# Attention, then a feed-forward layer: two further step orders, a fourth conversion buffer, a weight chunk asked for one period earlier

## The chip, the core and the metric

The kernel runs on one core of a Trainium2 chip. The metric is device time in microseconds (us). The engines are PE (TensorE), DVE (VectorE), ACT (ScalarE) and POOL (GpSimd); SP (SyncE) issues nearly all transfers. Each works through a queue of its own in the order in which the program was written, and waits at semaphores for what the others make.

## What is computed

```python
scores = 1/8 * matmul(q, k.T)                       # batch 8, heads 8, 576 tokens, head size 64
thresh = max(scores, -1) - tau                      # tau = 0.02
scores = where(scores >= thresh, scores, -1e9)
attn   = exp(scores - max(scores)); attn /= sum(attn) + 1e-9
x      = matmul(attn, v)                            # bridged to 4608 x 512
out    = maximum(x @ w_in, 0) ** 2 @ w_out          # 512 -> 2048 -> 512
```

q, k and v are float32. The two weight matrices come as float64, which the kernel takes as pairs of 32-bit words and turns into float32 itself.

## The kernel before

The first part of the run is attention, the rest is the feed-forward layer, which multiplies blocks with a scheme that needs sums of weight blocks beforehand. All of the change lies in the attention part.

**Units and periods.** Two heads form a pair (64 x 2 columns). 128 query rows of a pair, or the 64 leftover rows of two pairs, are a unit; there are 144 of them. A *period* p handles two units, A = 2p and B = 2p+1, so 72 periods are needed. A period's work is cut into named steps (`steps`, line 695). They are:

- PE: `SA`, `SB` scores against 512 keys and `RA`, `RB` against the last 64 (L434); `T` turns of q and k (L398); `U`, `V`, `W` turns of the finished weights of the softmax (L380); `Q` spreads the inverse sums (L517); `PV` multiplies by v (L534).
- DVE: `topA0` to `topB1` (L452) copy scores from PSUM and take the maximum; `maskA0` to `maskB1` (L467) compare with the threshold, multiply and sum, with two inputs in SBUF; `inv` (L477) is the reciprocal; `c4` (L227) and `c5` (L235) are two steps of a weight conversion; in periods without a conversion DVE also does half of `x` (L666).
- ACT: `powA0` to `powB1` (L462) are the exponentials; `eU`, `eV`, `eW` (L525) and `eT` (L403, L411) bring PE's turns from PSUM to SBUF; `x` (L664) copies the result; `c1` (L205) takes the absolute value of a chunk's high words.
- POOL: `leastA`, `leastB` (L459) make the thresholds; `over` (L474) adds 1e-9 to the sums; `xm` (L676) scales the result; `c2` (L212), `c3` (L219) and `c6` (L245) are conversion steps; `s1`, `s2` each do one sum of two weight blocks (L122, L125).
- SP: `fetch` (L191) asks for a chunk of raw weights; what `eT` and `xm` release is loaded and stored there too.

**The order.** Two strings list the steps: `CONVERTING` for the periods in which a weight chunk is in conversion (2 to 34) and `PLAIN` for the others; periods 0 and 1 have lists of their own (`BEGIN_WITH`, line 605). Each dash behind a name moves the step back by a period: `PV--` in period p is the `PV` of p-2. Since every engine works in order, the list fixes each engine's queue; waits between engines follow from the data, and from PSUM banks (`touch`, line 355: an access waits for the other engines' last one to the same bank). The scores use six banks: A's are 0 and 5, B's 2 and 3, the rests and the turns share 1 and 4; `W` and `Q` write to 2 and 3, `PV` to 0 and 5.

In the old plain order DVE does topB0, topB1, maskA1, x, inv, maskA0, maskB0, topA0, topA1, maskB1, and POOL s1, over, leastB, xm, s2, leastA. In the old converting order DVE does c5, topB1, c4, inv, topB0, maskA0, maskA1, topA0, topA1, maskB1, maskB0, and POOL c3, over, c6, leastB, xm, c2, leastA.

**Weight chunks.** 32 chunks are converted, one begun in each of the periods 2 to 33 (`starts`, line 564). A chunk's `fetch` stands two periods ahead of its `c1`; `c2` and `c3`, `c4`, `c5` and `c6` follow in that period and the next two. The raw words lie in one of four buffers, the absolute words (`a`, line 204) in one of three. From period 36 on `s1` and `s2` each make one sum, while there are any; `s2` only in periods before 60 (line 705).

Of the kernel before, what the change touches and what calls it, by code (L numbers as in the profile page):

```python
# [11 lines left out]
I32 = mybir.dt.int32  # L12
# [36 lines left out]
def kernel(  # L49
# [27 lines left out]
    P = 128  # L77
# [25 lines left out]
    sb, cv = Region(arena, 0, X_AT[0]), Region(arena, X_AT[0], ARENA)  # L103
# [49 lines left out]
    WC = 512  # L153
# [16 lines left out]
    blocks_out = [(m, k) for k in RAW for m in RAW]  # L170
    chunks += [(W_OUT, m, k, out_blocks[m, k]) for m, k in blocks_out[:EARLY]]
    is_wide = moe_w_in.dtype != FP32
    raws, parts = {}, {}

    def weight(m):
        return weight_tile(*chunks[m][0:3])

    def fetch(m):
        if m is None:
            return  # L180
        src = chunks[m][3]
        if not is_wide and m < 16:
            nc.sync.dma_start(out=weight(m)[:, :], in_=src)
            return
        raw = cv.tile([P, 2 * WC], I32, tag="raw", bufs=4, name="raw")
        if not is_wide:
            nc.sync.dma_start(out=raw[:, 0:WC].bitcast(FP32).rearrange("p (k o) -> p k o", k=4), in_=src)
            nc.sync.dma_start(out=slot_of(*chunks[m][1:3]), in_=raw[:, 0:WC].bitcast(FP32))
            return
        three = (lambda t: t.rearrange("p (k o) -> p k o", k=4)) if m >= 16 else (lambda t: t)  # L190
        nc.sync.dma_start(out=three(raw[:, :]), in_=src.bitcast(I32))  # L191
        raws[m] = raw

    def slot_of(m, k):
        return w_dram[ds((8 * raw_at(m) + raw_at(k)) * P, P), :]

    def pick(t, k):
        return t.rearrange("p (n two) -> p n two", two=2)[:, :, k]

    def convert1(m):  # L200
        if m not in raws:
            return
        lo, hi = pick(raws[m], 0), pick(raws[m], 1)
        a = cv.tile([P, WC], I32, tag="a", bufs=3, name="a")
        nc.scalar.activation(out=a.bitcast(FP32), in_=hi.bitcast(FP32), func=AF.Abs)  # L205
        parts[m] = (lo, hi, a)
        raws.pop(m)
# [280 lines left out]
    for g in range(2, 2 * len(pairs)):  # L488
        two, x = divmod(g - 4, 4)
# [9 lines left out]
    def fill(m, f, pt, at=None):  # L499

        first, count = FILLS[f]
        if m not in wT:
            wT[m] = sb.tile([P, (2 * CH + 2) * P], FP32, tag="wT", bufs=W_RING, name="wT")
        for i, (u, c) in enumerate(FIRST[first : first + count]):
            half_turn(pt, i, weights[2 * m + u][:, c, :, :].rearrange("p j d -> p (j d)"), at)
# [14 lines left out]
    def filled(m, f, pt, at=None):  # L520

        first, count = FILLS[f]
        count += 2 * (f == "W")
        to = wT[m][:, ds(weight_at(first) * P, count * P)]
        touch("weights", nc.scalar.copy(joined(to), whole(pt, 0, count)), at, 2 * BANK, m)  # L525
# [35 lines left out]
    def has(n):  # L561
        return 0 <= n < NU
# [5 lines left out]
    def sums_due(p):  # L568

        return p > max(starts) + 2 and not converts(p)  # L570

    def sums_step():
        while summing and next(summing[0], 0) == 0:
            summing.popleft()
# [10 lines left out]
    def converts(p):  # L585
        return is_wide and (has_chunk(p) or has_chunk(p - 1))
# [4 lines left out]
    def begun(n):  # L591
        return starts.get(n)

    FIRST_PERIOD = -2
    PLAIN = """
        c5- U-- SB-- c6 c4- eU-- RB-- s1- PV-- powA0-- topB0-- over-- topB1-- c1 powA1-- c2- powB0--
        maskA1-- T- x-- eT- leastB-- inv-- xm-- maskA0-- V-- W-- eV-- c3- Q-- eW-- powB1-- SA- maskB0-- RA-
        s2- topA0- topA1- maskB1-- leastA- fetch
    """.split()
    CONVERTING = """  # L600
        RB- RA eT- c5- topB1- powA0- c3- over- powA1- c6- fetch PV- x- powB1- c4 inv- topB0- leastB- V- eV-
        SA T W- xm- maskA0- powB0- maskA1- topA0 Q- eW- topA1 c2- maskB1- c1 U eU maskB0- SB leastA s1 s2
    """.split()

    BEGIN_WITH = {
# [2 lines left out]
        maskB0 maskB1  # L608
        """.split(),
        1: """  # L610
        fetch SA RA RB SB T eT over topA0 topA1 leastA inv V topB0 topB1 leastB powA0 powA1 eV W Q powB0 eW
        maskA0 maskA1 powB1 maskB0 maskB1
        """.split(),
    }
# [4 lines left out]
    def middle():  # L619
        return sc[:, 2 * BANK : 4 * BANK].rearrange("p (r n) -> p r n", r=2)  # L620

    def period(p):

        A, B_, a, b = 2 * p, 2 * p + 1, 2 * p - 2, 2 * p - 1
        m, turns = p - 2, TURNS.get(p, ())
        late, pt = {"W": []}, {}

        def fills(f, m):
            if has(2 * m):
                pt[f] = pt_pool.tile([P, 2, BANK], FP32, tag="pt", name="pt")  # L630
                fill(m, f, pt[f])

        def evict(f, m):
            if has(2 * m):
                filled(m, f, pt[f], 2 * BANK if f == "W" else None)

        def W():
            if has(2 * m + 2):
                pt["W"] = middle()
                fill(m + 1, "W", pt["W"], 2 * BANK)  # L640

        def Q():
            if has(2 * m + 2):
                spread_sums(m + 1, pt["W"], 2 * BANK)

        def turn_some():
            free = None
            if turns and p < 2:
                pq = pt_pool.tile([P, 2, BANK], FP32, tag="pt", name="pq")
                free = [(pq[:, r, :], None) for r in range(2)]  # L650
            late["turn"] = [turn(g // 2, g % 2, free or spots()) for g in turns]

        def PV():
            if has(2 * m):
                values(m)

        def values_out():
            if not has(2 * m):
                return
            late["x"] = x = sb.tile([P, 2, P], FP32, tag="x", bufs=2, name="x")  # L660
            for j in range(2):
                from_ = sc[:, ds(5 * j * BANK, P)]
                if converts(p) or j == 0:
                    made = nc.scalar.copy(x[:, j, :], from_)  # L664
                else:
                    made = nc.vector.tensor_tensor(  # L666
                        out=x[:, j, :], in0=from_, in1=wT[m][:, ts(SCALE_AT + j, P)], op=ALU.mult
                    )
                touch("x", made, 5 * j * BANK, P, m)

        def given_out():
            if has(2 * m):
                x = late.pop("x")
                made = x[:, 0 : 1 + converts(p), :].rearrange("p j n -> p (j n)")
                scale = wT[m][:, ds(SCALE_AT * P, (1 + converts(p)) * P)]
                nc.gpsimd.tensor_tensor(out=made, in0=made, in1=scale, op=ALU.mult)  # L676
                wT.pop(m)
                valued(m)
                give_x(m, x)
            ask(False)  # L680

        def scored(n):
            if has(n):
                scores(n, False)
                softmax(n)

        def scored_rest(n):
            if has(n):
                scores(n, True)

        def every(key):
            for then in late.get(key, ()):
                then()

        steps = {
            "U": lambda: fills("U", m), "V": lambda: fills("V", m + 1), "W": W, "Q": Q, "T": turn_some,
            "eU": lambda: evict("U", m), "eV": lambda: evict("V", m + 1), "eW": lambda: evict("W", m + 1),
            "eT": lambda: every("turn"),
            "SA": lambda: scored(A), "SB": lambda: scored(B_),
            "RA": lambda: scored_rest(A), "RB": lambda: scored_rest(B_),  # L700
            "PV": PV, "x": values_out, "xm": given_out,
            "c1": lambda: convert1(begun(p)), "c2": lambda: convert2(begun(p)),
            "c3": lambda: convert3(begun(p)), "c4": lambda: convert4(begun(p - 1)),
            "c5": lambda: convert5(begun(p - 1)), "c6": lambda: convert6(begun(p - 1)),
            "s1": lambda: sums_due(p) and sums_step(), "s2": lambda: sums_due(p) and p < 60 and sums_step(), "fetch": lambda: fetch(begun(p + 2)),
        }
        steps["over"] = lambda: do(a, "over")
        steps["inv"] = lambda: do(a, "inverse")
        for letter, n in (("A", A), ("B", B_)):
            for what, name in (("least", "least"),):  # L710
                steps[what + letter] = lambda n=n, name=name: do(n, name)
            for what, name in (("top", "top"), ("pow", "power"), ("mask", "mask")):
                for j in range(2):
                    steps[f"{what}{letter}{j}"] = lambda n=n, name=name, j=j: do(n, name, j)
        return steps
# [644 lines left out]
```

## Time and profile before

| what | value |
|---|---|
| three runs | 1295.56, 1300.23 and 1300.02 us, median 1300.02 |
| the profiled execution | 1296.16 us, of which the span is 1294.2 us |
| granted TensorE clock | 0.999 of full speed |
| PE busy | 1267.6 us, 98% of the span |
| DVE busy | 1000.9 us, 77% |
| ACT busy | 848.7 us, 66% |
| POOL busy | 1022.8 us, 79% |
| last reciprocal of the attention part | starts at 498.2 us |

The span runs from the first to the last instruction of the profiled execution; the run's own time is a little longer. "Busy" leaves out waiting, but an instruction that is held up after its start, for instance because another engine uses the same way to memory, counts as busy for all of its time. So one reads not only the gaps but also how long an operation takes in different places. In rows of the order in time, the columns are start, duration, engine, line, operation, output and input, shapes, count.

### The profile page before, as it was taken

How to read it: one execution, taken by the hardware profiler on the slowest of the kernel's cores; microseconds unless marked ns; L12 is line 12 of the kernel's file. 1: busy time of each engine (PE TensorE's matmuls, PEld its weight loads, DVE VectorE, ACT ScalarE, POOL GpSimd, SP SyncE). 2: the span in 40 equal slices, each digit the busy share in tenths (PEclk: the TensorE clock that was granted, in tenths of full speed). 3: DMA queues.
4: the chain of work that ended last, by engine and by line, in shares of the span. 5: the costliest groups of instructions: out<-in, count | busy, mean ns of one | idle time of the engine just before them, and what ended most of it. 6: DMA issues, size and time to landing. Idle time of an engine off the chain costs nothing.

```text
span 1294.2 us, 46028 instructions
## 1 busy us (share of the span) xinstructions
PE 1267.6 (98%) x18287; PEld 1103.2 (85%) x18287; DVE 1000.9 (77%) x2384; ACT 848.7 (66%) x1537; POOL 1022.8 (79%) x1070
## 2 busy tenths in 40 slices
PE   8999899999999999999999999999999999999998
PEld 5666666677777778988888888999999999999998
DVE  6999999999999995886887877877645654665463
ACT  6999999999999994666765766666523432443240
POOL 3999999988998542988897988758777867777775
PEclk9999999999999999999999999999999999999999
DMA  6655666444333312658767867589554324522411
GB/s 155 173 159 140 170 175 192 133 97 111 88 83 84 93 33 61 209 170 232 211 187 212 242 168 217 167 315 392 186 155 165 94 74 159 164 71 98 160 34 33
DMA packets 291414, 196.21 MB, mean 152 GB/s; under 512 B 100096, under 2 KB 252160, under 8 KB 291200
## 3 DMA queue, kind: packets, MB, share of 16 engines
q1 hardware_dynamic: 289888, 192.87, 51.3%
q8 instruction: 144, 2.36, 0.8%
q14 instruction: 70, 0.57, 0.1%
q10 hardware_dynamic: 1312, 0.41, 0.1%
HBM read 120.85 MB, written 72.35 MB: 149 GB/s over the span
## 4 chain that ended last, share of the span: by engine, by line
PE 68%; DVE 10%; DMA 7%; ACT 7%; issue 5%; POOL 2%; SPq 1%; DVEq 0%; ACTq 0%; POOLq 0%
PE po L1094 28%; PE ph L952 13%; PE sc L434 7%; PE ph L959 7%; PE sc L534 6%; DVE arena L452 4%; PE pt L380 3%; DVE arena L467 3%; DMA wall<-w 2%; ACT arena L525 2%; PE sc L398 1%; ACT arena L462 1%; PE sc L517 1%; DMA arena<-g 1%; DMA g<-arena 1%
## 5 line engine op out<-in xcount | busy, mean ns | idle before, releaser
L125 POOL TENSOR_TENSOR arena<-arena 128x512 f32<-128x512 f32 (+1 forms) x314 | 377.7, 1221 | 138.6 <-DVE arena L125 114.9
L1094 PE MATMUL po<-wall,arena 128*128 128x128 f32 x3528 | 395.2, 275 | 1.9 <-ACT arena L769 1.4
L1094 PEld LDWEIGHTS po<-wall,arena 128*128 128x128 f32 x3528 | 394.4, 192 | 2.6 <-ACT arena L769 1.8
L125 DVE TENSOR_TENSOR arena<-ph,arena 128x512 f32<-128x512 f32 x378 | 255.1, 689 | 79.0 <-PE ph L952 31.7
L122 POOL TENSOR_TENSOR arena<-arena 128x128 f32<-128x128 f32 (+1 forms) x322 | 265.8, 827 | 24.4 <-DMA arena<-w 8.8
L952 PE MATMUL ph<-arena,wall 128*128 128x256 f32 x1176 | 256.5, 380 | 2.2 <-DVE arena L125 1.8
L952 PEld LDWEIGHTS ph<-arena,wall 128*128 128x128 f32 x1176 | 222.2, 190 | 36.2 <-DVE arena L125 6.3
L467 DVE SCALAR_TENSOR_TENSOR arena<-arena 128x576 f32<-128x576 f32 x288 | 238.7, 848 | 3.4 <-ACT arena L462 0.5
L125 DVE TENSOR_TENSOR arena<-po,arena 128x128 f32<-128x128 f32 x378 | 108.3, 290 | 167.6 <-PE po L1094 163.1
L462 ACT ACTIVATE arena<-arena 128x576 f32<-128x576 f32 x288 | 216.0, 795 | 4.0 <-DVE arena L452 3.8
L808 ACT COPY c<-arena 128x512 f32<-128x512 f32 (+1 forms) x295 | 169.0, 578 | 73.7 <-DVE arena L122 35.8
L452 DVE TENSOR_SCALAR_CACHE_REDUCE arena<-sc 128x576 f32<-128x576 f32 x288 | 207.1, 747 | 8.5 <-ACT arena L525 3.4
L434 PE MATMUL sc<-arena 64*64 64x512 f32 (+1 forms) x2304 | 188.2, 418 | 7.9 <-ACT arena L403 1.5
L459 POOL TENSOR_SCALAR arena<-arena,tau_p 128x2 f32<-128x2 f32 x144 | 124.7, 866 | 78.4 <-DVE arena L452 71.5
L534 PE MATMUL sc<-arena 64*64 64x128 f32 (+1 forms) x5760 | 165.4, 260 | 0.1
L122 DVE TENSOR_TENSOR arena<-arena,c 128x512 f32<-128x512 f32 x235 | 154.4, 666 | 12.2 <-ACT c L808 8.7
L525 ACT COPY arena<-pt 128x1024 f32<-128x1024 f32 x144 | 146.9, 1020 | 7.3 <-PE pt L380 6.5
L534 PEld LDWEIGHTS sc<-arena 64*64 64x64 f32 x5760 | 150.4, 133 | 0.9 <-issue 0.4
L434 PEld LDWEIGHTS sc<-arena 64*64 64x64 f32 x2304 | 78.5, 133 | 83.5 <-issue 35.4
L769 ACT COPY arena<-po 128x128 f32<-128x128 f32 x63 | 16.6, 264 | 186.5 <-PE po L1094 183.7
L959 PE MATMUL ph<-arena,wall 128*128 128x128 f32 x1176 | 132.0, 275 | 0.6 <-DVE arena L666 0.6
L959 PEld LDWEIGHTS ph<-arena,wall 128*128 128x128 f32 x1176 | 131.6, 192 | 0.9 <-issue 0.7
(54 smaller groups left out, 1140.8 us busy)
## 6 DMA issues: line engine op xcount, KB each, us to landing
arena<-g SPq DMA_DIRECT2D x144, 256.0 KB, 4.5
g<-arena SPq DMA_DIRECT2D x192, 128.0 KB, 2.9
w<-arena SPq DMA_DIRECT2D x60, 256.0 KB, 2.6
wall<-w SPq DMA_DIRECT2D x49, 256.0 KB, 5.2
g<-arena SPq DMA_DIRECT2D x48, 256.0 KB, 3.6
arena<-w SPq DMA_DIRECT2D x44, 256.0 KB, 3.3
arena<-in_v_dram SPq DMA_DIRECT2D x32, 288.0 KB, 4.3
out_dram<-arena SPq DMA_DIRECT2D x70, 128.0 KB, 2.5
```

Of the source, the lines that this page charges most:

```text
L122: e.tensor_tensor(out=out, in0=x, in1=y, op=ALU.subtract)
L125: e.tensor_tensor(out=out, in0=x, in1=y, op=ALU.add)
L434: made = nc.tensor.matmul(sc[at, ds(to, count)], lhs, kT[rows, ds(at_k, count)], start=True, stop=True)
L452: made = nc.vector.tensor_scalar(out=s[:, j, :], in0=sc[:, ds(at, S)], scalar1=1.0, scalar2=None, op0=ALU.mult, op1=ALU.min, accum_out=nmx ...
L462: nc.scalar.activation(out=w[:, :, j, :], in_=of(j), func=AF.Exp, bias=nmx[:, j : j + 1], scale=-1.0)
L467: nc.vector.scalar_tensor_tensor(out=w[:, :, j, :], in0=of(j), scalar=thr[:, j : j + 1], in1=w[:, :, j, :], op0=ALU.is_le, op1=ALU.mult, a ...
L525: touch("weights", nc.scalar.copy(joined(to), whole(pt, 0, count)), at, 2 * BANK, m)
L534: made = nc.tensor.matmul(sc[ds(u * D, D), ds(5 * j * BANK + row, count)], loaded_v[i][rows, (c - (u != j)) % CH, :], wT[m][rows, ds(weigh ...
L808: nc.scalar.copy(c, y)
L952: nc.tensor.matmul(to[:, 2 * j : 2 * j + 2, :], W_IN[m, k][:, ts(2 * h + j, P)], part_x(steps, k, m), start=(not more and j == 0), stop=Tr ...
L959: nc.tensor.matmul(to[:, j, :], W_IN[m, k][:, ts(j, P)], x, start=(not more and j == 0), stop=True, skip_group_check=True,)
L1094: nc.tensor.matmul(to, g[:, j, :], w[:, j, :], start=(not more and j == 0), stop=(j == 3), skip_group_check=True)
```

## The change

Both lists of steps are replaced. A chunk's `c1` moves to the head of the converting period, so the absolute words get a fourth buffer. In period 1 a new step, `next`, asks for the chunk that would otherwise be asked for in period 2; `fetch` leaves out what has been asked for.

```diff
-    raws, parts = {}, {}
+    raws, parts, asked_for = {}, {}, set()
...
     def fetch(m):
-        if m is None:
+        if m is None or m in asked_for:
             return
+        asked_for.add(m)
...
-        a = cv.tile([P, WC], I32, tag="a", bufs=3, name="a")
+        a = cv.tile([P, WC], I32, tag="a", bufs=4, name="a")
...
     PLAIN = """
-        c5- U-- SB-- c6 c4- eU-- RB-- s1- PV-- powA0-- topB0-- over-- topB1-- c1 powA1-- c2- powB0--
-        maskA1-- T- x-- eT- leastB-- inv-- xm-- maskA0-- V-- W-- eV-- c3- Q-- eW-- powB1-- SA- maskB0-- RA-
-        s2- topA0- topA1- maskB1-- leastA- fetch
+        s2- PV-- x-- T-- V-- W-- c2 SA- c3- maskA0-- xm-- inv-- Q-- eT-- RB- maskB0-- topA0- c1- eV-- U-
+        topA1- leastA- eW-- SB- powB1-- maskB1-- eU- RA topB0- c4 topB1- s1 powA1- leastB- maskA1- over- c5
+        powA0- c6 powB0- fetch
     """.split()
     CONVERTING = """
-        RB- RA eT- c5- topB1- powA0- c3- over- powA1- c6- fetch PV- x- powB1- c4 inv- topB0- leastB- V- eV-
-        SA T W- xm- maskA0- powB0- maskA1- topA0 Q- eW- topA1 c2- maskB1- c1 U eU maskB0- SB leastA s1 s2
+        SB- c1 RA topB0- powA1- c2- topB1- PV- c5- powA0- maskA0- eT- leastB- over- V- x- T powB0- SA RB W-
+        maskA1- c3 c4 inv- Q- c6- fetch topA0 eV- topA1 leastA U xm- maskB0- powB1- eW- eU maskB1- s1 s2
     """.split()
...
         1: """
-        fetch SA RA RB SB T eT over topA0 topA1 leastA inv V topB0 topB1 leastB powA0 powA1 eV W Q powB0 eW
+        fetch next SA RA RB SB T eT over topA0 topA1 leastA inv V topB0 topB1 leastB powA0 powA1 eV W Q powB0 eW
...
+            "next": lambda: fetch(begun(p + 3)),
```

## The prediction

> **What bounds the kernel now.** The two orders steer only the attention half, so I read its stages first: busy time by stretch, then the reciprocal (L477), which runs once in each period.
>
> ```profile
> 32.10:249.60 217.50, 207.76 (x5188) 146.46 (x5188) 211.25 (x570) 203.65 (x370) 204.24 (x210) 1.00 0.60 164
> 277.00:430.70 153.70, 153.13 (x4126) 116.80 (x4124) 149.74 (x434) 145.46 (x246) 134.85 (x142) 1.00 0.39 91
> 430.70:493.50 62.80, 62.63 (x1692) 47.64 (x1686) 61.94 (x181) 58.32 (x95) 28.76 (x46) 1.00 0.26 59
> ```
> ```profile
> L477 DVE RECIPROCAL arena<-arena x9: 178/178/180, 89.2 to 146.3; 128x4 f32<-128x4 f32 x9
> L477 DVE RECIPROCAL arena<-arena x25: 160/170/175, 277.0 to 430.7; 128x4 f32<-128x4 f32 x25
> L477 DVE RECIPROCAL arena<-arena x12: 160/169/174, 430.7 to 498.2; 128x4 f32<-128x4 f32 x12
> ```
>
> The columns are PE, weight loads, DVE, ACT, POOL. DVE is busy for 97 to 99% of each stretch, and PE for 99.6% where no chunk is converted. A converting period takes (146.3-89.2)/8 = 7.1 us, a plain one with two weight sums (276.98 to 430.67) 153.7/24 = 6.40, later ones with at most one about 6.3. No idle time waits to be collected; an order gains or loses by how long the instructions themselves get. In the converting stage that is POOL and DVE against each other:
>
> ```profile
> 95.18 0.61 POOL L219 TENSOR_SCALAR arena<-arena 128x512 f32<-128x512 f32 x1
> 95.82 0.43 DVE L227 TENSOR_SCALAR arena<-arena 128x512 int32<-128x512 int32 x1
> 95.87 0.47 POOL L474 TENSOR_SCALAR arena<-arena 128x4 f32<-128x4 f32 x1
> 96.37 0.18 DVE L477 RECIPROCAL arena<-arena 128x4 f32<-128x4 f32 x1
> 96.42 1.04 POOL L245 TENSOR_TENSOR wall<-arena 128x512 int32<-128x512 int32 x1
> 97.12 0.95 DVE L467 SCALAR_TENSOR_TENSOR arena<-arena 128x576 f32<-128x576 f32 x1
> 99.49 1.64 POOL L212 TENSOR_SCALAR arena<-arena 128x512 int32<-128x512 uint32 x1
> 100.10 0.81 DVE L467 SCALAR_TENSOR_TENSOR arena<-arena 128x576 f32<-128x576 f32 x1
> 100.84 0.81 DVE L467 SCALAR_TENSOR_TENSOR arena<-arena 128x576 f32<-128x576 f32 x1
> 101.58 0.69 DVE L235 SCALAR_TENSOR_TENSOR arena<-arena 128x512 int32<-128x512 int32 x1
> 102.18 0.75 DVE L452 TENSOR_SCALAR_CACHE_REDUCE arena<-sc 128x576 f32<-128x576 f32 x1
> ```
>
> c4 (95.82) starts 0.03 after c3 ends (95.79), the reciprocal 0.03 after "over" ends (96.34): DVE waits for POOL twice. The mask at 97.12 takes 0.95 beside c6, those at 100.10 and 100.84 take 0.81 though c2 runs through one and into the other. In the plain stage the sums lie like this:
>
> ```profile
> 334.61 0.28 DVE L666 TENSOR_TENSOR arena<-sc,arena 128x128 f32<-128x128 f32 x1
> 334.82 0.17 DVE L477 RECIPROCAL arena<-arena 128x4 f32<-128x4 f32 x1
> 334.90 0.79 DVE L467 SCALAR_TENSOR_TENSOR arena<-arena 128x576 f32<-128x576 f32 x1
> 335.73 0.45 POOL L676 TENSOR_TENSOR arena<-arena 128x128 f32<-128x128 f32 x1
> 335.80 1.00 DVE L467 SCALAR_TENSOR_TENSOR arena<-arena 128x576 f32<-128x576 f32 x1
> 336.15 1.78 POOL L122 TENSOR_TENSOR wall<-wall 128x512 f32<-128x512 f32 x1
> 336.90 0.76 DVE L452 TENSOR_SCALAR_CACHE_REDUCE arena<-sc 128x576 f32<-128x576 f32 x1
> 337.58 0.75 DVE L452 TENSOR_SCALAR_CACHE_REDUCE arena<-sc 128x576 f32<-128x576 f32 x1
> 338.26 0.82 DVE L467 SCALAR_TENSOR_TENSOR arena<-arena 128x576 f32<-128x576 f32 x1
> 339.20 1.28 POOL L125 TENSOR_TENSOR wall<-wall 128x512 f32<-128x512 f32 x1
> ```
>
> A sum takes 1.28 beside tops (339.20), which read PSUM. The other one (336.15) meets a mask first and takes 1.78: it ends at 337.93, 1.13 after that mask (336.80). So a mask and a POOL operation exclude each other. Who wins when POOL waits and a second mask follows, one place shows, and two more show the same with c3 and c6 against c5 and c4:
>
> ```profile
> 257.62 0.78 DVE L467 SCALAR_TENSOR_TENSOR arena<-arena 128x576 f32<-128x576 f32 x1
> 257.73 1.27 POOL L676 TENSOR_TENSOR arena<-arena 128x256 f32<-128x256 f32 x1
> 258.34 1.28 DVE L467 SCALAR_TENSOR_TENSOR arena<-arena 128x576 f32<-128x576 f32 x1
> ```
> ```profile
> 159.61 1.08 POOL L219 TENSOR_SCALAR arena<-arena 128x512 f32<-128x512 f32 x1
> 160.15 1.10 DVE L235 SCALAR_TENSOR_TENSOR arena<-arena 128x512 int32<-128x512 int32 x1
> 161.42 1.04 POOL L245 TENSOR_TENSOR arena<-arena 128x512 int32<-128x512 int32 x1
> 161.84 0.90 DVE L227 TENSOR_SCALAR arena<-arena 128x512 int32<-128x512 int32 x1
> ```
>
> The waiting xm ends 0.60 after the first mask (258.40 to 259.00), and the second mask is 0.47 longer than 0.81: POOL goes first, and DVE pays about POOL's remaining run less 0.13. c5 pays 0.41, c4 0.47.
>
> **The change part by part.** No work is added or removed; per period each engine has the same instructions. Pitches (start to next start) from the rows: top 0.68 (336.90 to 337.58), mask 0.74 (100.10 to 100.84), c5 0.60, x 0.21, reciprocal 0.08, c4 about 0.36 (0.43 less the usual 0.07 of overlap).
>
> *Plain order, two sums (24 periods; `s2` runs for periods 36 to 59).* DVE's new order is x, maskA0, inv, maskB0, topA0, topA1, maskB1, topB0, topB1, maskA1: 0.21+4x0.74+0.08+4x0.68 = 5.97 bare. POOL's is s2, xm, leastA, s1, leastB, over. Take x at 0. leastA waits for topA1; s1 fits beside topB0 and topB1 as the sum at 339.20 does (1.28 against 2x0.68), with at most 0.1 into maskA1. leastB needs topB1, so it ends with maskA1, where the next x begins; "over" follows (0.47 above) and is done about when maskA0 begins. Now s2 has nothing to wait for but the port. It stands behind maskA0, gets in when that ends, and runs 1.13 (the end of the 1.78 row) against maskB0, which starts 0.08 later. maskB0 pays 1.13-0.13-0.08 = 0.92. Before, s2 came behind the second of the neighbouring masks and ran beside tops, for nothing. xm then waits behind s2 and maskB0 and ends beside a top, so the 0.2 that it costs a mask now is gone. Sum 5.97+0.92+0.05 (s1 into maskA1) = 6.94 against 6.40: +0.54 x 24 = **+13 us**. The next topA0, everything behind it on DVE and PE's next score step are late by this; PE, whose 6.3 bound the period before, waits instead. Bounds of the stretch, which no row shows for this pair: the 0.47 that the half-sized xm cost, giving 6.49 (+2), and a whole sum of 1.28 less 0.08, giving 7.22 (+20). I take 0.92, as the run of 1.13 is that of the same instruction. Below these bounds lies only the case in which the mask wins (first rival).
>
> *Converting order (31 periods in steady state).* DVE: topB0, topB1, c5, maskA0, maskA1, c4, inv, topA0, topA1, maskB0, maskB1; bare 4x0.68+4x0.74+0.60+0.36+0.08 = 6.72 against 7.13. c3 now belongs to a chunk one period younger than c4's, so c4 no longer waits for it: that stall goes. Late next is the port again. POOL has c2, leastB, over, c3, c6, leastA, xm. "over" and c3 meet maskA1 and c4 (0.1 to 0.25), c6 follows c3 beside the two tops A and reaches into maskB0 (the 0.95 row shows 0.14; up to 0.35). xm still ends beside topB0, and c2 beside topB1 and c5. Sum 6.72+0.15+0.2 = 7.07, so 0.06 x 31 = **-2 us**; from both ends 6.95 to 7.3, which is -6 to +5. PE's loop is shorter: inv, Q, eW, the B scores, the rest of A, topB0 come to about 6.5 by their rows, an estimate, and do not decide.
>
> *Plain periods without a second sum (12).* eW now stands between Q and the B scores on one loop with PE, where before the A scores covered it (Q's 0.46 and eW's 0.62 with their hand-overs come to about 1.2, against some 1.1 of PE's own work between the two; an estimate): 0.1 a period, +1 us, 0 to +3.
>
> ```profile
> 335.35 0.46 PE L517 MATMUL sc<-ident,arena 64*64 64x64 f32 x16
> 336.52 0.62 ACT L525 COPY arena<-sc 128x512 f32<-128x512 f32 x1
> ```
>
> *Fourth buffer and early request.* c1 moves to the head of a period. The fetch stands behind c6 as before, and its c1 comes two periods later:
>
> ```profile
> 97.48 0.34 SPq L191 DMA_DIRECT2D arena<-in_moe_w_in_dram  x1
> ...
> 98.97 0.69 ACT L205 ACTIVATE arena<-arena 128x512 f32<-128x512 f32 x1
> ```
> ```profile
> DMA to landing us min/median/max: 3.7/4.2/7.4
> ```
>
> That was 98.97+2x7.13-97.48 = 15.7 us of lead. In the new order c6 ends about 5.8 into a period and c1 starts one about 0.3 early, which leaves 14.1-0.3-5.8 = 8, and 7 behind SP's other issues. So the load is still hidden by those periods, barely for the slowest; were it not, ACT would stand with c1 ahead of all four powers, up to 0.4 us in such a period. The fourth buffer keeps c1 off a buffer that c6 and its store still hold; with three, c1 would wait for them. "next" adds no transfer: one issue moves a period earlier, past SP's other loads, worth between a gain of 0.5 us and a loss of 0.5; I take 0, since the pipeline is still filling there.
>
> **Sum:** -2+13+1 = +12 at 1294.2 span, or 1296.16 us for that execution: 1308. The three runs shown have their median 3.9 above it, so against 1300.0 I predict 1312. If all bounds above fall on one side, this case alone reaches from 1300-4 = 1296 to 1300+28 = 1328.
>
> On the Trainium skill: "SBUF — State Buffer", section "SBUF: two separate sides", says that VectorE operations with two SBUF inputs and GpSimd operations take a shared port pair exclusively, whoever starts first for its whole instruction. The 1.28 mask behind xm agrees; the two masks of 0.81 beside c2 do not. By the page c2 would also hold c5, which is the second rival.
>
> **The rivals.** *The mask wins (faster).* If, with inv between, maskB0 takes the port ahead of the waiting s2, then s2 runs beside the tops A and costs nothing. The two-sum periods then go to PE's 6.3 (-2), and the same preference would spare c4 and maskB0 part of what I charge them in the converting stage: 7.0 to 6.8, -2 to -11. That makes 1287 to 1296. For: one place alone shows two masks in a row against a big POOL operation. Against: all three places went POOL's way. It decides as soon as s2 costs maskB0 under 0.1 us. *c2 holds c5 (slower still).* c2 starts behind xm, about 0.8 into the period, and c5 comes at 1.36; if c2 keeps the port for the rest of its 1.6, c5 pays up to 0.9, and the converting stage gains nothing: 0.3 to 0.9 x 31 = 9 to 28 more, on 1314: 1323 to 1342. It decides as soon as c5 takes over 1.0. Against: masks beside c2 are not longer at all. *Nothing changes.* The stretches only move between the same engines, and each stage stays at its sum: 1297 to 1304.
>
> **How the numbers follow.** The forecast has 0.53, the mask wins 0.20, c2 holds c5 0.14, nothing changes 0.13. 0.5% is 6.5 us, about what a measurement of this kernel can tell from no change: faster below 1293.5, slower above 1306.5. Faster 0.14 (two thirds of the first rival). Same 0.20 (the third, the rest of the first, 0.01 of the forecast's low end). Slower 0.66 (the rest of the forecast, and c2's case). The range of 8 in 10 reaches from the first rival's middle, 1292, to the forecast's upper bound, 1328; left out are half of the first rival (0.10) and most of c2's case (0.10).
>
> **What would show it.** Right: between the reciprocals of the two-sum stage about 6.9 us; there the mask behind the reciprocal takes about 1.7 instead of 0.8, L122 and L125 on POOL lie half beside masks, and PE is busy for under 95%. In the converting stage about 7.1, c4 no longer at c3's end. Wrong: masks in that stage under 1.0 on average, or c5 over 1.0, or ACT idle before L205 behind a DMA.

## The result, and the profile after

The changed kernel took 1311.45 us (median of four runs, 1309.89 to 1312.85), the one before 1299.51 (four runs, 1295.56 to 1300.23): a ratio of 1.0098, 95% interval 1.0072 to 1.0124. The forecast of 1312 and its sign hold. The profiled execution took 1310.12 us, with a span of 1308.3. (The medians lie 11.9 us apart; the two profiled spans below lie 14.1 apart, since the old kernel's profile is of an execution of 1296.16 us, below its median.)

In the changed kernel the lines of the steps stand one further down: the fetch is L192, c1 L206, the top L453, the mask L468, the reciprocal L478, xm L677, `over` L475, c4 L228. The busy time by stretch, cut at the same reciprocals as before (columns again PE, weight loads, DVE, ACT, POOL):

```profile
36.60:243.90 207.30, 199.70 (x5176) 149.19 (x5176) 203.91 (x571) 201.60 (x368) 190.78 (x211) 1.00 0.61 167
271.90:442.90 171.00, 162.30 (x4122) 114.34 (x4114) 168.21 (x433) 150.79 (x246) 136.15 (x142) 1.00 0.37 86
```

The first row spans 30 converting periods, as the row of 217.50 did before: 10.2 us less, 6.91 in place of 7.25 a period. (Most old periods took 7.13; two longer ones make the mean, and more is said of them below.) The second spans the 24 periods with two sums: 171.0 against 153.7, so 17.3 us more, 7.12 in place of 6.40. DVE is still full (168.21 of 171.00), but PE has fallen from 99.6% to 94.9%: it waits for DVE there (7.3 of its 8.7 us of idle time end with a top that frees the banks for the next scores). The remaining pieces are a first converting reciprocal at 36.6 instead of 32.1 (+4.4), the passage between the stages (+0.7), the periods behind (+0.6) and the feed-forward part (+1.2); with -10.2 and +17.3 they make up, but for rounding, the 14.1 by which the span grew.

So the net is small because two large moves of opposite sign partly cancel. Where the 17 us went, one two-sum period shows in the order of time (start, duration; DVE and POOL only, without the 0.08 readouts):

```profile
335.50 0.28 DVE L667 TENSOR_TENSOR arena<-sc,arena 128x128 f32<-128x128 f32 x1
...
335.70 0.80 DVE L468 SCALAR_TENSOR_TENSOR arena<-arena 128x576 f32<-128x576 f32 x1
335.79 0.80 POOL L475 TENSOR_SCALAR arena<-arena 128x4 f32<-128x4 f32 x1
...
336.63 0.18 DVE L478 RECIPROCAL arena<-arena 128x4 f32<-128x4 f32 x1
336.68 1.27 POOL L122 TENSOR_TENSOR wall<-wall 128x512 f32<-128x512 f32 x1
336.72 1.84 DVE L468 SCALAR_TENSOR_TENSOR arena<-arena 128x576 f32<-128x576 f32 x1
337.91 0.97 POOL L677 TENSOR_TENSOR arena<-arena 128x128 f32<-128x128 f32 x1
...
338.50 0.75 DVE L453 TENSOR_SCALAR_CACHE_REDUCE arena<-sc 128x576 f32<-128x576 f32 x1
...
340.79 1.28 POOL L125 TENSOR_TENSOR wall<-wall 128x512 f32<-128x512 f32 x1
```

Read it from the mask at 336.72: it takes 1.84, where its neighbours take 0.80, and s2 (336.68) began 0.04 ahead of it and ran its full 1.27. The 1.03 that it loses is not idle time in any view; it counts as busy. A few rows up is a second, smaller loss: `over`, four columns wide, takes 0.80 because it started 0.09 behind maskA0 and came out only when that was done, and the reciprocal needs its result. It starts 0.93 behind maskA0 instead of 0.74.

The converting period:

```profile
90.20 0.60 POOL L475 TENSOR_SCALAR arena<-arena 128x4 f32<-128x4 f32 x1
90.65 0.44 DVE L228 TENSOR_SCALAR arena<-arena 128x512 int32<-128x512 int32 x1
90.89 0.66 POOL L220 TENSOR_SCALAR arena<-arena 128x512 f32<-128x512 f32 x1
91.01 0.16 DVE L478 RECIPROCAL arena<-arena 128x4 f32<-128x4 f32 x1
...
91.52 1.03 POOL L246 TENSOR_TENSOR wall<-arena 128x512 int32<-128x512 int32 x1
...
92.50 0.81 DVE L468 SCALAR_TENSOR_TENSOR arena<-arena 128x576 f32<-128x576 f32 x1
...
94.74 1.67 POOL L213 TENSOR_SCALAR arena<-arena 128x512 int32<-128x512 uint32 x1
95.34 0.68 DVE L236 SCALAR_TENSOR_TENSOR arena<-arena 128x512 int32<-128x512 int32 x1
```

c4 (90.65) starts 0.24 ahead of c3 (90.89), the reciprocal starts 0.36 behind c4 as if nothing held it, c6 is over at 92.55 when the mask has hardly begun, and c5 takes 0.68 in the middle of c2. The same in groups over the 30 periods, changed kernel first, then the old one (count, busy us, mean ns, idle before):

```profile
L468 DVE SCALAR_TENSOR_TENSOR arena<-arena 128x576 f32<-128x576 f32 x120 | 93.1, 813 | 0.7 <-POOL arena L213 0.4 <-ACT arena L463 0.3
...
L236 DVE SCALAR_TENSOR_TENSOR arena<-arena 128x512 int32<-128x512 int32 x30 | 20.6, 686 | 0.0
```
```profile
L467 DVE SCALAR_TENSOR_TENSOR arena<-arena 128x576 f32<-128x576 f32 x120 | 97.0, 842 | 0.0
...
L235 DVE SCALAR_TENSOR_TENSOR arena<-arena 128x512 int32<-128x512 int32 x30 | 21.7, 723 | 0.0
...
L477 DVE RECIPROCAL arena<-arena 128x4 f32<-128x4 f32 x30 | 5.3, 177 | 3.4
```

Where a usual period gained is best read from pitches, start to next start. Two more rows of the old kernel, beside those that the prediction shows (c4 at 95.82, the reciprocal at 96.37, the mask at 97.12):

```profile
95.05 0.75 DVE L452 TENSOR_SCALAR_CACHE_REDUCE arena<-sc 128x576 f32<-128x576 f32 x1
...
98.00 0.81 DVE L467 SCALAR_TENSOR_TENSOR arena<-arena 128x576 f32<-128x576 f32 x1
```

The mask beside c6 has a pitch of 0.88 (97.12 to 98.00) instead of 0.74: 0.14. The top ahead of c4 has 0.77 (95.05 to 95.82) instead of 0.68, as c4 waits for c3: 0.09. c4 has 0.55 (95.82 to 96.37) instead of 0.36 (90.65 to 91.01), as the reciprocal waits for `over`: 0.19. Of these 0.42 the reciprocal and the top behind it give back 0.06. That leaves 0.36, the whole way from 7.13 to the 6.77 of the new period (91.01 to its next reciprocal at 97.78). A wait costs more here than its idle time, since the overlap with the instruction ahead is lost too. So a usual period of the old converting order paid for POOL in three places, and the new one, in the period shown, pays in none of them. No run takes the three apart.

c5's larger mean in the old kernel (723) isn't of that kind; its median is 694 against 685. It comes from the two long old periods, of 9.24 us (153.42 to 162.66) and 8.77 us (212.48 to 221.25), in which c5 took 1.10 and 1.09 and DVE stood idle before a top, for 1.43 and 0.99. The first of them:

```profile
157.30 0.76 DVE L452 TENSOR_SCALAR_CACHE_REDUCE arena<-sc 128x576 f32<-128x576 f32 x1 [1.43 <-ACT arena L525]
```

What the two periods take beyond 7.13 makes 3.7 of the 10.2 us. No experiment was aimed at them, and why they are long stays open.

### The profile page after: what moved, and what is told of

Read it like the earlier page. It is cut to its first block, busy times and chain, and to the rows that moved or that the text cites. A ratio compares the mean times of both kernels' runs of the same rounds, so it can differ in the third digit from the quotient of the medians.

```text
span 1308.3 us, 45977 instructions
## 1 busy us (share of the span) xinstructions
PE 1272.8 (97%) x18287; PEld 1104.7 (84%) x18287; DVE 1015.0 (78%) x2384; ACT 854.0 (65%) x1537; POOL 1016.6 (78%) x1070
## 3 DMA queue, kind: packets, MB, share of 16 engines
q10 hardware_dynamic: 1312, 0.41, 0.1%
## 4 chain that ended last, share of the span: by engine, by line
PE 71%; ACT 8%; DMA 6%; DVE 5%; issue 4%; POOL 4%; SPq 1%; DVEq 0%; POOLq 0%; ACTq 0%
PE po L1096 27%; PE ph L954 13%; PE ph L961 9%; PE sc L535 9%; PE sc L435 8%; ACT arena L526 3%; PE pt L381 2%; DVE arena L453 2%; ACT arena L463 2%; DMA g<-arena 2%; DMA arena<-xT 2%; DVE arena L468 1%; PE sc L399 1%; DVE arena L125 1%; DMA arena<-g 1%
## 5 line engine op out<-in xcount | busy, mean ns | idle before, releaser
L125 POOL TENSOR_TENSOR arena<-arena 128x512 f32<-128x512 f32 (+1 forms) x314 | 377.6, 1221 | 136.8 <-DVE arena L125 103.0
L125 DVE TENSOR_TENSOR arena<-ph,arena 128x512 f32<-128x512 f32 x378 | 255.1, 689 | 78.8 <-PE ph L954 30.9
L122 POOL TENSOR_TENSOR arena<-arena 128x128 f32<-128x128 f32 (+1 forms) x322 | 264.8, 823 | 27.4 <-DMA arena<-w 11.6
L468 DVE SCALAR_TENSOR_TENSOR arena<-arena 128x576 f32<-128x576 f32 x288 | 256.4, 908 | 1.7 <-ACT arena L463 1.2
L125 DVE TENSOR_TENSOR arena<-po,arena 128x128 f32<-128x128 f32 x378 | 108.3, 290 | 167.9 <-PE po L1096 163.6
L435 PE MATMUL sc<-arena 64*64 64x512 f32 (+1 forms) x2304 | 197.8, 423 | 16.8 <-DVE arena L453 8.6
L453 DVE TENSOR_SCALAR_CACHE_REDUCE arena<-sc 128x576 f32<-128x576 f32 x288 | 205.6, 750 | 8.8 <-PE sc L435 5.0
L460 POOL TENSOR_SCALAR arena<-arena,tau_p 128x2 f32<-128x2 f32 x144 | 102.2, 710 | 94.3 <-DVE arena L453 84.7
L122 DVE TENSOR_TENSOR arena<-arena,c 128x512 f32<-128x512 f32 x235 | 154.4, 666 | 13.3 <-ACT c L810 9.2
L435 PEld LDWEIGHTS sc<-arena 64*64 64x64 f32 x2304 | 75.7, 134 | 100.9 <-DVE arena L453 40.2
L535 PEld LDWEIGHTS sc<-arena 64*64 64x64 f32 x5760 | 148.7, 134 | 1.4 <-ACT arena L526 0.7
```

The lines of the kernel that those rows point to most:

```text
L122: e.tensor_tensor(out=out, in0=x, in1=y, op=ALU.subtract)
L125: e.tensor_tensor(out=out, in0=x, in1=y, op=ALU.add)
L435: made = nc.tensor.matmul(sc[at, ds(to, count)], lhs, kT[rows, ds(at_k, count)], start=True, stop=True)
L453: made = nc.vector.tensor_scalar(out=s[:, j, :], in0=sc[:, ds(at, S)], scalar1=1.0, scalar2=None, op0=ALU.mult, op1=ALU.min, accum_out=nmx ...
L468: nc.vector.scalar_tensor_tensor(out=w[:, :, j, :], in0=of(j), scalar=thr[:, j : j + 1], in1=w[:, :, j, :], op0=ALU.is_le, op1=ALU.mult, a ...
L535: made = nc.tensor.matmul(sc[ds(u * D, D), ds(5 * j * BANK + row, count)], loaded_v[i][rows, (c - (u != j)) % CH, :], wT[m][rows, ds(weigh ...
```

## The experiments

The theory for the plain order was the prediction's: s2 ahead of xm holds maskB0. Its rival: the new wait of the reciprocal for `over` delays the period. For the converting order: the gain is DVE's freedom from POOL, c4's from c3 above all. Its rivals: it comes from the early request, the fourth buffer or the place of c1. All ratios are against the kernel before, run on the same chip, with 95% intervals.

### E1: the second sum behind xm

```diff
-        s2- PV-- x-- T-- V-- W-- c2 SA- c3- maskA0-- xm-- inv-- Q-- eT-- RB- maskB0-- topA0- c1- eV-- U-
+        PV-- x-- T-- V-- W-- c2 SA- c3- maskA0-- xm-- inv-- Q-- eT-- RB- maskB0-- s2- topA0- c1- eV-- U-
```

> The changed kernel with s2 behind xm instead of ahead of it in POOL's queue; all other queues as they are. Theory (port: s2 holds maskB0 for about 1.0 us): xm takes the place behind maskA0 and costs maskB0 0.2 to 0.4, s2 then waits for maskB0 and runs beside the tops A; two-sum period 6.4 to 6.6 instead of 7.19, 14 to 18 us off, 1294 to 1298. Rival (the order of DVE and PE itself costs the time, through the reciprocal that waits for 'over' and PE's loop over Q and eW): period stays above 7.0, 1309 to 1313.

Measured: 1291.99 us, ratio 0.9959 (0.9938 to 0.9980). The 25 reciprocals of the two-sum stage, and the same stretch of a period:

```profile
L478 DVE RECIPROCAL arena<-arena x25: 177/178/179, 273.8 to 427.4; 128x4 f32<-128x4 f32 x25
```
```profile
337.73 0.18 DVE L478 RECIPROCAL arena<-arena 128x4 f32<-128x4 f32 x1
337.77 0.45 POOL L677 TENSOR_TENSOR arena<-arena 128x128 f32<-128x128 f32 x1
337.82 1.02 DVE L468 SCALAR_TENSOR_TENSOR arena<-arena 128x576 f32<-128x576 f32 x1
...
338.19 1.79 POOL L122 TENSOR_TENSOR wall<-wall 128x512 f32<-128x512 f32 x1
```

153.6/24 = 6.40: all of the 17 us is gone by moving one POOL instruction behind another. xm is now what precedes the mask and costs it 0.21 (1.02-0.81); s2 comes second, waits for the mask (1.79 instead of 1.27) and runs beside tops, where nobody waits for it. The reciprocal still starts 0.93 behind maskA0 here, so the rival can't be the main part.

### E2: the addition of 1e-9 earlier

```diff
-        topA1- leastA- eW-- SB- powB1-- maskB1-- eU- RA topB0- c4 topB1- s1 powA1- leastB- maskA1- over- c5
+        topA1- leastA- eW-- SB- powB1-- maskB1-- eU- RA topB0- c4 topB1- s1 over- powA1- leastB- maskA1- c5
```

> The changed kernel with 'over' ahead of leastB in POOL's queue of the plain order, so that the reciprocal never waits for it; s2 keeps its place ahead of xm. Theory (port): s2 still asks for the port among the masks, at maskA0 instead of maskB0; only the reciprocal's wait of 0.1 to 0.2 goes: period 6.9 to 7.2, 1305 to 1312. Rival (the reciprocal's wait for 'over' is what costs the time): period 6.4, 1294.

Measured: 1307.83 us, ratio 1.0083 (1.0056 to 1.0109).

```profile
L478 DVE RECIPROCAL arena<-arena x25: 165/167/174, 272.2 to 440.9; 128x4 f32<-128x4 f32 x25
```
```profile
335.31 0.83 DVE L468 SCALAR_TENSOR_TENSOR arena<-arena 128x576 f32<-128x576 f32 x1
...
336.07 0.17 DVE L478 RECIPROCAL arena<-arena 128x4 f32<-128x4 f32 x1
336.18 1.27 POOL L122 TENSOR_TENSOR wall<-wall 128x512 f32<-128x512 f32 x1
336.25 1.82 DVE L468 SCALAR_TENSOR_TENSOR arena<-arena 128x576 f32<-128x576 f32 x1
```

The reciprocal now follows maskA0 at once (0.76), and the mask is as long as ever. 168.7/24 = 7.03 against 7.12: the wait was worth 0.1 a period, the sum 0.7. The rival is a side effect.

### E7: half of the second sum ahead of the mask, half behind

```diff
-            yield op(nc.gpsimd, to[:, :], W[m, x][:, :], W[m, y][:, :])
+            yield in_parts(op, to, W[m, x], W[m, y])
...
+    def in_parts(op, to, x, y):
+        of = lambda a, n: op(nc.gpsimd, to[:, ds(a, n)], x[:, ds(a, n)], y[:, ds(a, n)])
+        if not halved[0]:
+            return of(0, BANK)
+        rest_of.append(lambda: of(BANK // 2, BANK // 2))
+        return of(0, BANK // 2)
...
-        s2- PV-- x-- T-- V-- W-- c2 SA- c3- maskA0-- xm-- inv-- Q-- eT-- RB- maskB0-- topA0- c1- eV-- U-
+        s2- PV-- x-- T-- V-- W-- c2 SA- c3- maskA0-- xm-- inv-- Q-- eT-- RB- maskB0-- s3- topA0- c1- eV-- U-
```

`halved[0]` is true only while `s2` runs: `s2` makes the first 256 columns at its old place, the new step `s3` the others behind xm.

> The changed kernel with s2's sum cut into two halves of 256 columns: the first where s2 stands, the second behind xm, beside the tops A. Theory (port): maskB0 pays for the half alone, about 0.4 instead of 1.03, and xm then waits for maskB0: two-sum period 6.5 to 6.7, 1296 to 1301. Rival (an instruction of any size at this place costs a turn of the queue): period 7.1 or more, 1310 or more.

Measured: 1297.45 us, ratio 1.0005 (0.9994 to 1.0016). In this kernel the reciprocal is L487, the mask L477.

```profile
L487 DVE RECIPROCAL arena<-arena x25: 177/177/179, 269.5 to 429.5; 128x4 f32<-128x4 f32 x25
```
```profile
342.58 0.73 POOL L122 TENSOR_TENSOR wall<-wall 128x256 f32<-128x256 f32 x1
342.63 1.30 DVE L477 SCALAR_TENSOR_TENSOR arena<-arena 128x576 f32<-128x576 f32 x1
```

160.0/24 = 6.67. Together with E1 and the changed kernel this gives three doses at one place, `xm`, half a sum and a whole one: POOL runs of 0.45, 0.73 and 1.27 that begin 0.04 to 0.05 ahead of the mask lengthen it from 0.81 by 0.21, 0.49 and 1.03. The cost is POOL's run less 0.24 each time.

### E3 and E4: each order alone

```diff
     PLAIN = """
-        s2- PV-- x-- T-- V-- W-- c2 SA- c3- maskA0-- xm-- inv-- Q-- eT-- RB- maskB0-- topA0- c1- eV-- U-
...
+        c5- U-- SB-- c6 c4- eU-- RB-- s1- PV-- powA0-- topB0-- over-- topB1-- c1 powA1-- c2- powB0--
...
```
```diff
     CONVERTING = """
-        SB- c1 RA topB0- powA1- c2- topB1- PV- c5- powA0- maskA0- eT- leastB- over- V- x- T powB0- SA RB W-
...
+        RB- RA eT- c5- topB1- powA0- c3- over- powA1- c6- fetch PV- x- powB1- c4 inv- topB0- leastB- V- eV-
...
```

The old plain order with the rest of the change:

> The new converting order with the old plain order (fourth buffer and early request kept). If the parts add up: two-sum period 6.40, later ones 6.29, the converting stage as in the changed kernel, 6.9: 1311.5-17-1 = 1293 to 1294. If the gain in the converting stage came only with the new plain order's phase: 1299 or more.

The old converting order with the rest of the change:

> The old converting order with the new plain order (fourth buffer and early request kept). If the parts add up: converting periods 7.13 to 7.25, the first periods shorter by 4 us as before, two-sum period 7.1 to 7.2: 1311.5+10-4 = 1317 to 1318.

Measured: 1289.28 us, ratio 0.9945 (0.9924 to 0.9966), with the old plain order; 1319.90 us, ratio 1.0164 (1.0138 to 1.0190), with the old converting order. Their reciprocals in the two stages, E3 first:

```profile
L478 DVE RECIPROCAL arena<-arena x31: 156/158/165, 35.2 to 244.0; 128x4 f32<-128x4 f32 x31
...
L478 DVE RECIPROCAL arena<-arena x25: 161/169/173, 269.4 to 423.1; 128x4 f32<-128x4 f32 x25
```
```profile
L478 DVE RECIPROCAL arena<-arena x31: 172/178/179, 31.8 to 248.4; 128x4 f32<-128x4 f32 x31
...
L478 DVE RECIPROCAL arena<-arena x25: 177/178/179, 278.8 to 449.8; 128x4 f32<-128x4 f32 x25
```

E3 has 208.8/30 = 6.96 and 153.7/24 = 6.40, E4 216.6/30 = 7.22 and 171.0/24 = 7.12. The orders act separately: the converting one is worth -0.55% of the time, the plain one +1.64%, and both together +0.98%, all three with the fourth buffer and the early request. These two by themselves don't bring the gain: E4 has them, and 7.22 a period against 7.25 before.

### E12: c3 of the same chunk as c4

```diff
-        maskA1- c3 c4 inv- Q- c6- fetch topA0 eV- topA1 leastA U xm- maskB0- powB1- eW- eU maskB1- s1 s2
+        maskA1- c3- c4 inv- Q- c6- fetch topA0 eV- topA1 leastA U xm- maskB0- powB1- eW- eU maskB1- s1 s2
```

> The changed kernel with c3 for the same chunk as the c4 behind it, as before the change, instead of for the next chunk: c4 must wait for the c3 that POOL does just before. If the converting stage gains from the c4 that no longer waits: converting period 6.8 back to 7.1 or up to 7.6, 1319 to 1335. If the gain comes from elsewhere (mask and c6 no longer meet, 'over' earlier): within 3 us of the changed kernel, 1309 to 1315.

Measured: 1358.19 us, ratio 1.0474 (1.0454 to 1.0494), more than expected.

```profile
L478 DVE RECIPROCAL arena<-arena x31: 163/165/167, 37.1 to 293.9; 128x4 f32<-128x4 f32 x31
```
```profile
94.92 0.61 POOL L220 TENSOR_SCALAR arena<-arena 128x512 f32<-128x512 f32 x1
95.50 1.04 POOL L246 TENSOR_TENSOR wall<-arena 128x512 int32<-128x512 int32 x1
95.57 1.25 DVE L228 TENSOR_SCALAR arena<-arena 128x512 int32<-128x512 int32 x1 [0.79 <-POOL arena L220]
...
100.23 0.76 DVE L453 TENSOR_SCALAR_CACHE_REDUCE arena<-sc 128x576 f32<-128x576 f32 x1 [0.52 <-issue]
```

256.8/30 = 8.56 a period. c4 waits 0.79 for c3, is then behind c6 in time (95.50 against 95.57) and takes 1.25 instead of 0.44; the reciprocal and with it PE come late, and the next top stands idle 0.52. One dependency that ends just where POOL begins its next long instruction costs twice. The granted clock of this stretch is 0.91 against 1.00 in the changed kernel, so part of the 47 us may be the clock's; the masks there take no longer than before (median 808 ns), and c4's wait for c3 and its 1.25 are DVE's and POOL's. So the new order needs a c3 that is a period older than its c4. It doesn't show that this wait was the most of what the old order lost: there it cost 0.09 a period, by the pitches above.

### E5 and E6: the early request, and the fourth buffer

```diff
-        fetch next SA RA RB SB T eT over topA0 topA1 leastA inv V topB0 topB1 leastB powA0 powA1 eV W Q powB0 eW
+        fetch SA RA RB SB T eT over topA0 topA1 leastA inv V topB0 topB1 leastB powA0 powA1 eV W Q powB0 eW
```

> The changed kernel without the early request. Theory: it only moves one issue while the pipeline fills; within 2 us of the changed kernel, 1309 to 1313, the third reciprocal at 36 to 37 us as in it. Rival (the early request causes the later start of 4 us by pushing SP's other loads back): third reciprocal at 32 to 33, 1307.

```diff
-        a = cv.tile([P, WC], I32, tag="a", bufs=4, name="a")
+        a = cv.tile([P, WC], I32, tag="a", bufs=3, name="a")
```

> The changed kernel with three buffers for the absolute words. For the second 16 chunks c6 writes its result into that buffer and a store reads it, so c1 at the head of the third period after must wait for the landing, some 2 us with four powers behind it: 16 x 1 to 2.5 = 16 to 40 us more, 1327 to 1351. For the first 16 chunks c5 is the last reader, long done: nothing. Rival (the store is landed in time): within 2 us of the changed kernel.

Measured: E5 1314.90 us, ratio 1.0134 (1.0115 to 1.0153); E6 1343.30 us, ratio 1.0341 (1.0316 to 1.0367). The waits of ACT's c1 (L206): E5 between 24 and 110 us, then E6 between 130 and 260 (us in total, times, longest).

```profile
ACT arena L206 <- DMA arena<-in_moe_w_in_dram: 3.5, 3, 2.5
```
```profile
ACT arena L206 <- DMA w<-arena: 21.8, 7, 5.5
```

The changed kernel has one wait of the first kind in that stretch, of 0.4. Without the request c1, which now heads a period, waits for its raw words and all four powers wait with it. The load wait is shown; the timed worth of the request, 0.36% between the two medians, has intervals that overlap. With three buffers c1 waits for the store of the chunk begun three periods earlier, whose buffer it needs, as the prediction said. The granted clock of E6's converting stretch (35.5 to 280.8) is 0.92, so how much of its time is the wait's alone isn't shown. The buffer is needed by this order, and by itself makes nothing faster (E4).

### E9: another list for period 2

The late first reciprocal (36.6) was to be mended with E3 and a list of its own for the first converting period.

```diff
+        2: """
+        SA RA RB c1 topA0 topA1 leastA SB U eU T c3
+        """.split(),
```

> The new converting order with the old plain order, and a list of its own for period 2: scores of A ahead of the turns, scores of B right behind, so that DVE doesn't stand idle while the new order starts. If the later start is due to the turns and U standing ahead of the scores in period 2: third reciprocal at 32 to 33 instead of 35 to 36.5, 3 us off the version without this list, 1286. Rival (the later start is due to loads): no change from 1289.

Measured: 1291.44 us, ratio 0.9959 (0.9942 to 0.9975), against E3's 0.9945: no gain.

```profile
L478 DVE RECIPROCAL arena<-arena x31: 156/158/164, 36.3 to 244.9; 128x4 f32<-128x4 f32 x31
```

The first of these reciprocals is at 36.3, later than E3's at 35.2. This list doesn't mend the late start; the theory that the order inside period 2 makes it has nothing for it.

### E10: c1 later in the period

```diff
-        SB- c1 RA topB0- powA1- c2- topB1- PV- c5- powA0- maskA0- eT- leastB- over- V- x- T powB0- SA RB W-
+        SB- RA topB0- powA1- c2- topB1- PV- c5- powA0- maskA0- eT- c1 leastB- over- V- x- T powB0- SA RB W-
```

Also on E3.

> The version with the new converting order and the old plain order, with c1 behind eT instead of at the head of the period, so that each weight load has some 2 us more before its c1. If the waits of c1 for late loads (2.5 us in that version, up to 0.9 each) still cost time: 2 to 4 us less than its 1289, 1285 to 1287, and no idle time of ACT before c1. If c1 is better at the head (the powers behind it come later for the masks, or c3 waits for it): 1289 or more.

Measured: 1292.14 us, ratio 0.9966 (0.9955 to 0.9977).

```profile
L478 DVE RECIPROCAL arena<-arena x31: 157/158/160, 36.1 to 247.9; 128x4 f32<-128x4 f32 x31
```

211.8/30 = 7.06 against E3's 6.96, though no c1 waits for a load any more. In these traces c1 at the head costs less than c1 between the copies of the turns; the intervals of the two times overlap.

### E11: E1 and E2 together

> The changed kernel with both edits of POOL's queue in the plain order: s2 behind xm, and 'over' ahead of leastB. Theory (port): xm asks beside x, before maskA0, and costs one mask 0.2 to 0.4, s2 then waits for masks and runs beside the tops A, and the reciprocal waits for nothing: two-sum period 6.2 to 6.4, 1289 to 1292. Rival (s2 gets in between maskA0 and maskB0, since xm is done earlier): period 7.0, 1307.

Measured: 1288.47 us (1287.88 to 1290.91), ratio 0.9939 (0.9922 to 0.9956), faster than both kernels and level with E3.

```profile
L478 DVE RECIPROCAL arena<-arena x31: 157/158/160, 36.8 to 243.5; 128x4 f32<-128x4 f32 x31
...
L478 DVE RECIPROCAL arena<-arena x25: 165/174/178, 269.3 to 422.1; 128x4 f32<-128x4 f32 x25
```

206.7/30 = 6.89 and 152.8/24 = 6.37: the new converting order's gain, and a new plain order without its loss.

## Why the prediction was right, and where it was not

**Plain order, two sums: right in mechanism, short in size** (+13 us, measured +17.3). Forecast 6.94 a period; the period shown takes 7.19, the mean is 7.12. Three terms make up the difference. maskB0 was charged 0.92 and pays 1.78-0.74 = 1.04 (338.50-336.72, against the bare pitch). The run of 1.13 was mis-sized: it came from a sum that had already waited for a mask, while here POOL starts first and runs 1.27. The reciprocal was charged nothing for `over`, though the text put its end "about when maskA0 begins"; it began 0.09 behind that and cost 0.19. And s1 into maskA1 was charged 0.05 and cost nothing. 6.94+0.12+0.19-0.05 = 7.20, which is the period shown; the mean is 0.07 lower because the last two of these 24 intervals (6.36 and 6.47) are done in periods 60 and 61, without a second sum: `inv` belongs to the unit pair begun two periods earlier. s2 also did not "get in" between two waiting masks as told: POOL was at `over` until 0.09 behind the first mask, and s2 then began 0.04 ahead of the second.

**Converting order: right in sign, wrong in size** (-2 us, measured -10.2, outside the bounds of -6 to +5). The forecast took 7.13 as the old period; against that the mean of 6.91 saves 6.5 in 30 periods, and the other 3.7 are the excess of the two long old periods, which it left out. The bare sum of 6.72 was good; most periods take 6.7 to 6.9. What failed are the two charges of 0.15 and 0.2 for "over", c3 and c6 against maskA1, c4 and maskB0: all three POOL operations fell beside tops or came behind a mask or a c4 that had already begun, and these weren't lengthened (masks 813 ns on average over 120, c4 0.44). The prediction took a meeting in time for a cost; who starts first is what counts. Nor was the c4 wait the main stall: by the pitches it cost 0.09 a period, the reciprocal's wait for `over` 0.19 and the longer mask 0.14. The mean of 6.91 is above that since seven of the last nine periods take 7.1 to 7.4; c1's waits for loads are part of it (1.6 us in two of these periods, below), the rest stays open.

```profile
ACT arena L206 <- DMA arena<-in_moe_w_out_dram: 1.6, 2, 0.9
```

**Plain periods without a second sum:** +1, measured +0.6 from the last two-sum reciprocal to the last of all (67.5 us before, 68.2 after). Whether the loop over eW that the prediction named makes it, no run shows.

**Fourth buffer and early request.** The buffer did what was said (E6). "Hidden, barely for the slowest" is what three waits of c1 show (0.4, 0.7 and 0.9), up to twice the 0.4 named. "next" was taken as 0 within 0.5; E5 has 3.5 us of waits without it. What failed there is that a still filling pipeline hides a late load: with c1 at the head of the period it didn't hide these.

**The start** was no term of the sum. The first converting reciprocal is 4.4 us late, of which some 2 us are only its later place in the period: in E3 the passage to the old plain order is 25.4 us long (244.0 to 269.4) against 27.35 before (249.63 to 276.98). What remains, 1 us in E3 and up to 2.4 in the changed kernel, has an open cause after E9; it comes with the new converting order, since E4, with the old one, the buffer and the request, starts at 31.8. This, the larger loss and the larger gain happen to cancel: the terms -10.2, +17.3, +0.6 and the rest give +14.1 in the span where +12 was forecast. That the time was met within 1 us, better than any of its large parts, is luck; the sign and the larger part, the loss by s2, are not.

**The rivals.** *The mask wins:* refuted, 1.84; though no run has a mask and a waiting POOL operation that become free at one moment, since POOL was ahead by 0.04 to 0.07 in the rows shown. *c2 holds c5:* refuted, c5 takes 686 ns on average in the middle of c2. *Nothing changes:* refuted by both stages, though the total came near it.

**The signs named beforehand:** the mask at about 1.7 (1.84), PE under 95% (94.9%) and c4 off c3's end are there. Half of the sums lie beside a mask, as named: each s2 begins just ahead of maskB0 (336.68), each s1 runs beside tops (340.79). The two lines are differences (L122) and sums (L125), and both steps have some of each. The forecast's 6.9 a period is 7.12, its 7.1 in the converting stage is 6.91. One of the signs of being wrong is there too, ACT idle before c1 behind a DMA, for 2.0 us in all.

## What to carry to other kernels

When an engine's order is changed, write down not only which instructions overlap but which of two that hold each other up starts first: the later one pays, and a long one that starts just ahead of a critical one can cost nearly its whole run (not every pair does, as c2 shows). Put the shortest instruction of the off-path engine there and the long one behind it (E1: one step moved, about 18 us by the two ratios). And time the stages of a kernel separately, since a result near zero may be two changes worth keeping apart.

## What the runs showed of the hardware

A two-input DVE operation of 128x576 in SBUF was lengthened by a POOL operation on two tensors that began 0.04 to 0.05 us earlier by that one's run less 0.24 us, for runs of 0.45, 0.73 and 1.27 us. c4, with one input, was held in the same manner by c6 (1.25 instead of 0.44). Yet c2, a POOL conversion from uint32 to int32 of 1.67 us, lengthened neither masks (0.81 in the old kernel, whose rows the prediction shows) nor c5 (0.68). The rule of the Trainium skill that the prediction weighed ("SBUF — State Buffer", section "SBUF: two separate sides": whoever starts first has the port pair for its whole instruction) is borne out by the three doses, but for the 0.24, and not by c2. A POOL operation on four columns takes about as long as the rest of the mask that it meets, here 0.80 and 0.60, since it ends 0.09 and 0.08 behind that mask (336.59 against 336.50; 90.80 against 90.72).
